# A state-space convolution beside a feed-forward: raw buffers of their own, a gate block in two halves, and loads ahead for the last convolution step

## The chip, the cores and the metric

The kernel runs on one NeuronCore of a Trainium2 chip. Five engines run their own instruction streams in order: TensorE (PE; its weight loads are shown apart as PEld), VectorE (DVE), ScalarE (ACT), GpSimd (POOL) and SyncE (SP), which here only issues DMAs. The metric is device time in microseconds. The measured times of the kernel before are 1185.72, 1187.77 and 1189.12 us, median 1187.77 us.

## The reference

The input u has 2048 rows of 576 channels, in float32. Each row is layer-normalised to xn. Two branches read xn, and the result is their sum with the input:

```python
x = A_u
xn = _layernorm(x, axis=-1)
return x + _A_ref(xn, ...) + _B_ref(xn, B_w1, B_w2)
```

Branch A is a long convolution. For each channel a kernel K of 2048 taps is built from 128 complex exponentials (`K = einsum("dn,dnl,dn->dl", C, exp(dt*A*l), dt*B).real`), K and xn are padded to 4096, multiplied in the frequency domain and transformed back, and `xn * Dskip` is added. Branch B is a feed-forward layer, `silu(xn @ w1) @ w2`, with 4608 hidden units.

## The kernel before

**Numbers.** Products are made at more than one float32r pass: an operand is split into a high part (a copy rounded to float32r, on ACT) and a low part (the subtraction of the two, on DVE), and three matmuls (high x high, high x low, low x high) make one product. The code names the parts h and l (`w1h`, `w1l`, `w2h`, `w2l`, `xh`, `xl`, `gh`, `gl`).

**Phase 0** (`phase0`, `norm`, `normed`, `put_xt`). The 2048 rows are 16 tiles of 128, j = 0 to 15. For each pair of tiles x is loaded (L156), the statistics are made on DVE (L170, L171), a power on POOL (L175) gives the inverse deviation, and xn is written by DVE for even j (L179) and by ACT for odd j (L184). PE transposes xn (L118, L122); ACT and DVE write the split transposed tiles (L119, L120, L123, L124). Four tiles make a block of 512 tokens with its `xts` entry: j = 0 to 3 are block b=0, j = 4 to 7 block b=1 of the first half. The tiles 8 to 15 are transposed too and kept in DRAM (`dxt`) for the second half. xn itself goes to DRAM (`dxn`) for the convolution.

**Feed-forward** (`ffn`). The hidden units are nine chunks of four tiles (FT = 4). For each half of the tokens and each chunk there are two blocks of 512 tokens, 36 blocks in all. `load_w1` and `load_w2` load weights in pairs of tiles, through a raw buffer (`w1r`, `w2r`, one of each), and split them. `up(blk, t)` makes one tile of the gate: 14 matmuls of 512 columns into a PSUM bank (L262 to L264), SiLU on ACT (L268), the copy to `gh` (L269) and the subtraction to `gl` (L270). `down(blk, jj)` makes one token tile of the output: 24 matmuls of 288 columns (L285) and two additions into `acc[j]` on DVE (L288). After the first half, `acc` of j = 0 to 7 is stored in DRAM as `dr0`, and the buffers take x of j = 8 to 15.

**Convolution** (`side`). `natural` and `kgen` build K, `spread` transforms xn, and their results lie in DRAM (`d1k`, `d1u`). `spectral` makes 32 steps of products (L628) and stores each to `d2` (L600). The last step is `add_conv(j, dst)`: it loads `ys` from `d2` in two DMAs (L635; a `ys` needs rows of all 32 spectral steps), makes eight small matmuls into two PSUM banks (`py`, L645; in the trace each shows as more than one record) and adds them to the destination on DVE (L651). For j = 0 to 7 this is done in `tail`: a buffer `r0` is loaded from `dr0` (L606; the trace names it r), `add_conv` adds to it, and it is stored to the output in four DMAs (L161). For j = 8 to 15 `add_conv` is called in `down` of the last chunk and adds to `acc[j]`, which is stored at the very end.

**Order.** The program is traced as one list by `weave`, which runs the feed-forward as the main line, of 288 steps (one for each `up` or `down`), and puts each piece of the side line at the step given by its mark, a fraction of 288. The marks (L655) are 0.14 to 0.65 for the kernel and `spread`, 0.65 to 0.88 for `spectral`, and then to 0.94 for `tail`. A scheduler then gives each engine its order: earlier traced work goes first among what it takes to be ready by its own times. `tc.high_priority()` moves work ahead of all other, and `behind(ins)` keeps what is traced in its block, on the engine of `ins` alone, behind `ins` in that engine's order; it waits for no data. Buffers of a pool tag are limited by `bufs`; a tile waits until its buffer is free. SP issues its DMAs in the order given, so one that waits holds those behind it. `pins` keeps the instructions that `behind` refers to: `xt_s` and `xt_v` are the last ACT copy and DVE subtraction of a transposed tile (L123, L124).

Of the kernel before, what the change touches and what calls it, by code (L numbers as in the profile page):

```python
# [10 lines left out]
F32 = mybir.dt.float32  # L11
# [30 lines left out]
def kernel(  # L42
# [83 lines left out]
    xts = {}  # L126
    pins = {}

    def spread(up):
# [29 lines left out]
    def store(t, j, engines):  # L159
        for ps, v, eng in quarters(ov, engines):  # L160
            eng.dma_start(v[:, j], t[ps])  # L161
# [55 lines left out]
    def behind(ins):  # L217
        return tc.issue_after(ins) if ins is not None else nullcontext()

    def ffn():  # L220
        w2v = w2.rearrange("(t p) d -> p t d", p=P)
        blocks = [(half, c, b) for half in range(2) for c in range(NCH) for b in range(2)]
# [1 line left out]

        def load_w1(half, c, t):
            f = c * FT + t
            r1 = wp.tile([P, 5, 2 * P], F32, tag="w1r", name="w1r", bufs=1)
            fs = slice(f * P, (f + 2) * P)
            nc.sync.dma_start(r1[:, 0:4, :], w1[0:512, fs].rearrange("(k p) f -> p k f", p=P))
            nc.sync.dma_start(r1[0:64, 4, :], w1[512:576, fs])  # L230
            nc.sync.dma_start(r1[64:128, 4, :], w1[512:576, fs])
            for i in range(2):
                h1 = wp.tile([P, 5, P], F32R, tag="w1h", name="w1h", bufs=FT + 1)
                l1 = wp.tile([P, 5, P], F32R, tag="w1l", name="w1l", bufs=FT + 1)
                src = r1[:, :, i * P:(i + 1) * P]
                nc.scalar.copy(h1, src)  # L236
                with behind(pins["xt_v"] if f == half == 0 else None):
                    nc.vector.tensor_sub(l1, src, h1)  # L238
                W1[half, c, t + i] = h1, l1

        def load_w2(half, c, t):
            f = c * FT + t
            r2 = wp.tile([P, 2, D], F32, tag="w2r", name="w2r", bufs=1)
            nc.sync.dma_start(r2, w2v[:, f:f + 2, :])
            for i in range(2):
                h2 = wp.tile([P, D], F32R, tag="w2h", name="w2h", bufs=FT + 1)
                l2 = wp.tile([P, D], F32R, tag="w2l", name="w2l", bufs=FT + 1)
                with behind(pins["xt_s"] if f == half == 0 else None):
                    nc.scalar.copy(h2, r2[:, i, :])  # L249
                with behind(pins["xt_v"] if f == half == 0 else None):  # L250
                    nc.vector.tensor_sub(l2, r2[:, i, :], h2)  # L251
                W2[half, c, t + i] = h2, l2
                yield

        def up(blk, t):
            half, c, b = blk
            xh, xl, x4 = xts[2 * half + b]
            h1, l1 = W1[half, c, t]
            ph = ps1.tile([P, 512], F32, tag="ps1", name="ph")
            for n, (w, v) in enumerate(((h1, xh), (h1, xl), (l1, xh))):  # L260
                for kt in range(NKT):
                    nc.tensor.matmul(ph, w[:, kt, :], v[:, kt, :], start=n + kt == 0, stop=False)  # L262
            nc.tensor.matmul(ph, h1[:, 4, :], x4, start=False, stop=False)  # L263
            nc.tensor.matmul(ph, l1[:, 4, :], x4, start=False, stop=True)  # L264
            gf = gp.tile([P, 512], F32, tag="gf", name="gf", bufs=2)
            gh = gp.tile([P, 512], F32R, tag="gh", name="gh")
            gl = gp.tile([P, 512], F32R, tag="gl", name="gl")
# [3 lines left out]
            G[blk, t] = gh, gl  # L271

        def down(blk, jj):
            half, c, b = blk
            j = 8 * half + 4 * b + jj
            js = slice(jj * P, (jj + 1) * P)
            if half == 1 and c == NCH - 1:
                add_conv(j, acc[j])
            for h in range(2):
                hs = slice(h * HD, (h + 1) * HD)  # L280
                po = ps2.tile([P, 512], F32, tag="ps2", name="po")
                n = 0
                for t in range(FT):
                    for g, w in ((0, 0), (0, 1), (1, 0)):
                        nc.tensor.matmul(po[:, :HD], G[blk, t][g][:, js], W2[half, c, t][w][:, hs],  # L285
                                         start=n == 0, stop=n == 3 * FT - 1)
# [18 lines left out]

        for t in (0, 2):
            load_w1(0, 0, t)
            for _ in load_w2(0, 0, t):
                pass
        yield 0  # L310
        for t in range(FT):
            up(blocks[0], t)
            yield 3.0

        for i, blk in enumerate(blocks):
# [20 lines left out]
                    if k in (0, 2) and more and b == 0:  # L336
                        load_w1(*new, k)

    kl = yp = None
    kf = {}  # L340

    def natural(nat):
# [259 lines left out]

    def tail():
        for j in range(8):
            r0 = yp.tile([P, D], F32, tag="r0", name="r0")
            nc.sync.dma_start(r0, dr0[j * P:(j + 1) * P, :])  # L606
# [16 lines left out]
    def mm3(dst, terms, hs):  # L623

        n = 0
        for sh, sl, (mh, ml) in terms:
            for st, mv in ((sh, mh), (sh, ml), (sl, mh)):
                nc.tensor.matmul(dst, st, mv[:, hs], start=n == 0, stop=n == 3 * len(terms) - 1)  # L628
                n += 1

    def add_conv(j, dst):

        ys = yp.tile([P, 4, HD], F32, tag="ys", name="ys")
        for h in range(2):
            nc.sync.dma_start(ys[64 * h:64 * h + 64],  # L635
                              d2[j * 256:(j + 1) * 256, h * HD:(h + 1) * HD].rearrange("(q r) d -> r q d", q=4))
        first = None
        py = [pss.tile([P, 512], F32, tag="pss", name="py") for _ in range(2)]
        for q1 in range(2):
            for q2 in range(2):  # L640
                for h in (1, 0):
                    o = 64 * q1 + 32 * q2
                    rows = slice(64 * h, 64 * h + 64)
                    with tc.high_priority(), behind(first):
                        mm = nc.tensor.matmul(py[h][o:o + 32, :HD], s4[rows], ys[rows, 2 * q2 + q1],  # L645
                                              start=True, stop=True,
                                              tile_position=(64 * h, o), skip_group_check=True)
                    first = first or mm.ins
        for h in range(2):
            hs = slice(h * HD, (h + 1) * HD)  # L650
            nc.vector.tensor_add(dst[:, hs], py[h][:, :HD], dst[:, hs])  # L651

    def side():
        nonlocal s4, kl, yp
# [34 lines left out]

        def at_mark(at):  # L690
            k = int(at)
            return marks[k] + (at - k) * (marks[k + 1] - marks[k]) if k < 3 else marks[3]

        with tc.tile_pool(name="kl", bufs=2) as kl:
            for at in spectral():
# [92 lines left out]
```

## Time and profile before

| what | value |
|---|---|
| measured times, us | 1185.72, 1187.77, 1189.12; median 1187.77 |
| the profiled execution, us | 1184.91, of which the span is 1183.1 |
| mean granted TensorE clock | 0.987 |
| busy PE, DVE, ACT, POOL, us | 1132.1, 942.5, 699.0, 24.7 |
| first and last matmul start, us | 10.68, 1178.6 |
| last spectral store landed, first `ys` issued, us | 1096.0, 1096.84 |
| HBM read and written, MB | 102.63, 44.90 |

Times within the profile are microseconds from the start of the span. A busy PE is one that has a matmul in flight: matmuls are pipelined, so the start-to-start distance of neighbours is what one more of them costs, and the duration of one is longer. Where a row of a timeline holds several instructions (xN), its time reaches from the first start to the last end, and may hold waits. A wait is put down to what came last. The row of the granted clock is in tenths of full speed, over 40 equal slices of the span.

### The profile page before, as it was taken

Reading aid. Unit: us, or ns where it says so; the run is one execution under the profiler, and the core shown is the slowest. Engines: PE = TensorE matmul, PEld = TensorE weight load, DVE = VectorE, ACT = ScalarE, POOL = GpSimd, SP = SyncE. Lnnn points to the kernel's source line nnn. Section 1 sums busy time; section 2 is a strip of 40 time slices with the busy share of each in tenths; the row PEclk is TensorE's granted clock in tenths of the full one; section 3 lists DMA queues with packets and bytes.
Section 4 is the critical chain, followed back from the end, with each engine's and each line's share of the span. In section 5 each row is a group of like instructions: output and inputs, shape, how many; then the busy total and the mean of one; then the engine's idle time right before and its main releaser. Section 6 shows DMA issues by size and latency. Waiting matters only on the chain.

```text
span 1183.1 us, 22598 instructions
## 1 busy us (share of the span) xinstructions
PE 1132.1 (96%) x8984; PEld 1014.9 (86%) x8984; DVE 942.5 (80%) x1645; ACT 699.0 (59%) x1246; POOL 24.7 (2%) x42
## 2 busy tenths in 40 slices
PE   5999999999999999999999999999999999999958
PEld 3898889888888898998898889899989999999726
DVE  5798898999888989999899985488767878876223
ACT  3465556566565657665665654477767777776200
POOL 1100000000000000000000000000000000000000
PEclk9999999999999999999999999999999999999969
DMA  9356220505124242447451413654544544440895
GB/s 266 117 158 202 78 85 21 132 31 120 62 84 89 93 89 93 89 155 211 153 132 47 124 47 94 167 165 145 151 128 146 154 142 145 151 148 31 214 245 132
DMA packets 161625, 148.92 MB, mean 126 GB/s; under 512 B 82448, under 2 KB 124192, under 8 KB 161008
## 3 DMA queue, kind: packets, MB, share of 16 engines
q1 hardware_dynamic: 157088, 132.19, 39.7%
q0 software_dynamic: 3472, 13.53, 4.0%
q10 hardware_dynamic: 960, 1.77, 0.6%
q8 instruction: 70, 1.15, 0.4%
q14 instruction: 35, 0.29, 0.1%
HBM read 102.63 MB, written 44.90 MB: 125 GB/s over the span
## 4 chain that ended last, share of the span: by engine, by line
PE 65%; DMA 12%; DVE 11%; ACT 6%; issue 3%; SPq 2%; POOL 0%; ACTq 0%; DVEq 0%; POOLq 0%
PE po L285 27%; PE ph L262 23%; DMA w1r<-in_B_w_dram 3%; DMA d1u<-u 2%; PE kp L530 2%; DMA ys<-d 2%; PE pk L628 2%; PE pb L628 2%; PE pu L628 2%; PE z L542 2%; PE ph L263 2%; PE ph L264 2%; DVE acc L288 1%; DVE S L509 1%; DVE C L509 1%
## 5 line engine op out<-in xcount | busy, mean ns | idle before, releaser
L285 PE MATMUL po<-w2h,gh 128*128 128x288 f32 x1152 | 337.7, 299 | 6.8 <-ACT gh L269 5.9
L285 PE MATMUL po<-w2l,gh 128*128 128x288 f32 x1152 | 339.6, 297 | 0.4 <-issue 0.4
L285 PE MATMUL po<-w2h,gl 128*128 128x288 f32 x1152 | 333.9, 297 | 1.4 <-DVE gl L270 1.4
L285 PEld LDWEIGHTS po<-w2h,gh 128*128 128x128 f32 x1152 | 216.5, 189 | 16.9 <-ACT gh L269 6.8
L285 PEld LDWEIGHTS po<-w2l,gh 128*128 128x128 f32 x1152 | 217.8, 189 | 6.4 <-issue 2.0
L285 PEld LDWEIGHTS po<-w2h,gl 128*128 128x128 f32 x1152 | 215.7, 189 | 4.9 <-DVE gl L270 2.2
L262 PE MATMUL ph<-xh,w1h 128*128 128x512 f32 x576 | 161.6, 396 | 4.7 <-ACT gf L268 2.7
L262 PE MATMUL ph<-xl,w1h 128*128 128x512 f32 x576 | 160.2, 391 | 0.0
L262 PE MATMUL ph<-xh,w1l 128*128 128x512 f32 x576 | 159.8, 392 | 0.0
L288 DVE TENSOR_TENSOR acc<-po,acc 128x288 f32<-128x288 f32 x288 | 125.6, 451 | 28.4 <-PE po L285 27.1
L262 PEld LDWEIGHTS ph<-xh,w1l 128*128 128x128 f32 x576 | 107.0, 188 | 22.3 <-issue 1.4
L268 ACT ACTIVATE gf<-ph 128x512 f32<-128x512 f32 x144 | 85.7, 596 | 68.2 <-PE ph L264 43.9
L262 PEld LDWEIGHTS ph<-xl,w1h 128*128 128x128 f32 x576 | 106.7, 188 | 20.7
L262 PEld LDWEIGHTS ph<-xh,w1h 128*128 128x128 f32 x576 | 104.2, 189 | 23.2 <-ACT gf L268 3.7
L269 ACT CAST gh<-gf 128x512 fp32r<-128x512 f32 x144 | 88.1, 620 | 48.5 <-PE po L285 46.6
L270 DVE TENSOR_TENSOR gl<-gf,gh 128x512 fp32r<-128x512 f32 x144 | 97.9, 684 | 18.0 <-ACT gh L269 17.2
L236 ACT CAST w1h<-w1r 128x640 fp32r<-128x640 f32 x72 | 51.6, 724 | 72.6 <-DMA w1r<-in_B_w_dram 64.8
L238 DVE TENSOR_TENSOR w1l<-w1r,w1h 128x640 fp32r<-128x640 f32 x72 | 58.7, 820 | 25.1 <-ACT w1h L236 24.8
L249 ACT CAST w2h<-w2r 128x576 fp32r<-128x576 f32 x72 | 46.5, 672 | 26.3 <-DMA w2r<-in_B_w_dram 21.5
L251 DVE TENSOR_TENSOR w2l<-w2r,w2h 128x576 fp32r<-128x576 f32 x72 | 52.6, 751 | 8.9 <-ACT w2h L249 8.5
L489 ACT ACTIVATE c<-th,magic 128x1040 f32<-128x1040 f32 x36 | 41.9, 1165 | 29.9 <-DVE C L510 22.0
L264 PE MATMUL ph<-x,w1l 128*128 128x512 f32 x144 | 56.6, 393 | 0.0
(169 smaller groups left out, 1845.2 us busy)
## 6 DMA issues: line engine op xcount, KB each, us to landing
w2r<-in_B_w_dram SPq DMA_DIRECT2D x36, 576.0 KB, 3.9
w1r<-in_B_w_dram SPq DMA_DIRECT2D x36, 512.0 KB, 4.7
d1u<-u SPq DMA_DIRECT2D x32, 288.0 KB, 2.6
d1k<-stage SPq DMA_DIRECT2D x18, 512.0 KB, 8.0
ur<-d1u SPq DMA_DIRECT2D x32, 288.0 KB, 3.7
kr<-d1k SPq DMA_DIRECT2D x32, 288.0 KB, 2.9
d<-yo SPq DMA_DIRECT2D x32, 288.0 KB, 3.9
ys<-d SPq DMA_DIRECT2D x32, 288.0 KB, 5.6
```

Of the source, the lines that this page charges most:

```text
L236: nc.scalar.copy(h1, src)
L238: nc.vector.tensor_sub(l1, src, h1)
L249: nc.scalar.copy(h2, r2[:, i, :])
L251: nc.vector.tensor_sub(l2, r2[:, i, :], h2)
L262: nc.tensor.matmul(ph, w[:, kt, :], v[:, kt, :], start=n + kt == 0, stop=False)
L264: nc.tensor.matmul(ph, l1[:, 4, :], x4, start=False, stop=True)
L268: nc.scalar.activation(gf, ph, AF.Silu)
L269: nc.scalar.copy(gh, gf)
L270: pins["gl"] = nc.vector.tensor_sub(gl, gf, gh).ins
L285: nc.tensor.matmul(po[:, :HD], G[blk, t][g][:, js], W2[half, c, t][w][:, hs], start=n == 0, stop=n == 3 * FT - 1)
L288: nc.vector.tensor_add(acc[j][:, hs], po[:, :HD], acc[j][:, hs])
L628: nc.tensor.matmul(dst, st, mv[:, hs], start=n == 0, stop=n == 3 * len(terms) - 1)
```

## The change

- `load_w1` and `load_w2`: for the first chunk of the first half, the second pair (t = 2) takes its raw buffer from phase 0's pool `pa`, so it does not share with the first pair. The first pair's three w1 DMAs are issued by POOL instead of SP. Both w1 pairs are traced before both w2 pairs. The w1l subtractions of these pairs come behind the last DVE instruction of tile j = 1 (before: those of the first pair behind tile 3's), the w2h copies behind tile 3's last ACT copy for both pairs, and the w2l subtractions behind the last w1l.
- `up` takes a range of columns, and the first block is done as two halves, columns 0 to 255 of all four tiles and then 256 to 511 of all four.
- In `side`, the DVE work of tiles 4 to 7 comes behind the last DVE instruction of tile 3 (`pins["xt3"]`).
- `add_conv` no longer loads: `conv_load(j)` does, two steps ahead, into four buffers instead of three, and `tail_load` loads `r0` two steps ahead into three. The `py` matmuls lose their high priority; the first of each step comes behind the last feed-forward matmul traced (`pins["pe"]`).
- The marks become 0.14, 0.65, 0.875, 0.905, 0.945: `spectral` ends at 0.875, and step j of `tail` is traced at 0.905 + 0.005 j.

```diff
@@ load_w1, load_w2
-            r1 = wp.tile([P, 5, 2 * P], F32, tag="w1r", name="w1r", bufs=1)
+            first = half == 0 and f < FT
+            r1 = (pa if first and t else wp).tile([P, 5, 2 * P], F32, tag="w1r", name="w1r", bufs=1)
...
-            nc.sync.dma_start(r1[:, 0:4, :], w1[0:512, fs].rearrange("(k p) f -> p k f", p=P))
-            nc.sync.dma_start(r1[0:64, 4, :], w1[512:576, fs])
-            nc.sync.dma_start(r1[64:128, 4, :], w1[512:576, fs])
+            eng = nc.gpsimd if first and t == 0 else nc.sync
+            eng.dma_start(r1[:, 0:4, :], w1[0:512, fs].rearrange("(k p) f -> p k f", p=P))
+            eng.dma_start(r1[0:64, 4, :], w1[512:576, fs])
+            eng.dma_start(r1[64:128, 4, :], w1[512:576, fs])
...
-                with behind(pins["xt_v"] if f == half == 0 else None):
-                    nc.vector.tensor_sub(l1, src, h1)
+                with behind(pins["xt1"] if first else None):
+                    pins["w1l"] = nc.vector.tensor_sub(l1, src, h1).ins
...
-            r2 = wp.tile([P, 2, D], F32, tag="w2r", name="w2r", bufs=1)
+            r2 = (pa if first and t else wp).tile([P, 2, D], F32, tag="w2r", name="w2r", bufs=1)
...
-                with behind(pins["xt_v"] if f == half == 0 else None):
+                with behind(pins["w1l"] if first else None):
                     nc.vector.tensor_sub(l2, r2[:, i, :], h2)
@@ up
-        def up(blk, t):
+        def up(blk, t, a=0, e=512):
...
-                    nc.tensor.matmul(ph, w[:, kt, :], v[:, kt, :], start=n + kt == 0, stop=False)
+                    nc.tensor.matmul(ph, w[:, kt, :], v[:, kt, a:e], start=n + kt == 0, stop=False)
...
@@ down
             if half == 1 and c == NCH - 1:
+                conv_load(j + 2)
                 add_conv(j, acc[j])
@@ ffn
         for t in (0, 2):
             load_w1(0, 0, t)
+        for t in (0, 2):
             for _ in load_w2(0, 0, t):
                 pass
         yield 0
         for t in range(FT):
-            up(blocks[0], t)
+            up(blocks[0], t, 0, 256)
+        for t in range(FT):
+            up(blocks[0], t, 256, 512)
             yield 3.0
@@ tail
         for j in range(8):
-            r0 = yp.tile([P, D], F32, tag="r0", name="r0")
-            nc.sync.dma_start(r0, dr0[j * P:(j + 1) * P, :])
-            add_conv(j, r0)
-            store(r0, j, (nc.sync,))
-            yield 2 + (j + 1) / 8
+            if j < 2:
+                conv_load(j)
+                r0s[j] = tail_load(j)
+        for j in range(8):
+            yield 3 + j / 8
+            if j < 6:
+                r0s[j + 2] = tail_load(j + 2)
+            conv_load(j + 2)
+            add_conv(j, r0s[j])
+            store(r0s[j], j, (nc.sync,))
+
+    def tail_load(j):
+        r0 = yp.tile([P, D], F32, tag="r0", name="r0", bufs=3)
+        nc.sync.dma_start(r0, dr0[j * P:(j + 1) * P, :])
+        return r0
@@ add_conv
+    def conv_load(j):
+        if j < NJ:
+            yss[j] = yp.tile([P, 4, HD], F32, tag="ys", name="ys", bufs=4)
+            for h in range(2):
+                nc.sync.dma_start(yss[j][64 * h:64 * h + 64],
+                                  d2[j * 256:(j + 1) * 256, h * HD:(h + 1) * HD].rearrange("(q r) d -> r q d", q=4))
...
-                    with tc.high_priority(), behind(first):
+            with behind(first):
...
@@ side
-        marks = (0.14, 0.65, 0.88, 0.94)
+        marks = (0.14, 0.65, 0.875, 0.905, 0.945)
         with tc.tile_pool(name="pa", bufs=4) as pa:
             for js in ((0, 1), (2, 3), (4, 5), (6, 7)):
-                phase0(pa, js)
+                with behind(pins["xt3"] if js[0] > 2 else None):
+                    phase0(pa, js)
+                pins[f"xt{js[1]}"] = pins["xt_v"]
```

More of the change, by code (lines that the diff above doesn't have):

```diff
@@ L127, with behind @@
     pins = {}
+    def behind(ins):
+        return tc.issue_after(ins) if ins is not None else nullcontext()
     def spread(up):
@@ L242, in load_w2 @@
             f = c * FT + t
-            r2 = wp.tile([P, 2, D], F32, tag="w2r", name="w2r", bufs=1)
+            first = half == 0 and f < FT
+            r2 = (pa if first and t else wp).tile([P, 2, D], F32, tag="w2r", name="w2r", bufs=1)
             nc.sync.dma_start(r2, w2v[:, f:f + 2, :])
@@ L247, in load_w2 @@
                 l2 = wp.tile([P, D], F32R, tag="w2l", name="w2l", bufs=FT + 1)
-                with behind(pins["xt_s"] if f == half == 0 else None):
+                with behind(pins["xt_s"] if first else None):
                     nc.scalar.copy(h2, r2[:, i, :])
-                with behind(pins["xt_v"] if f == half == 0 else None):
+                with behind(pins["w1l"] if first else None):
                     nc.vector.tensor_sub(l2, r2[:, i, :], h2)
@@ L284, in down @@
                     for g, w in ((0, 0), (0, 1), (1, 0)):
-                        nc.tensor.matmul(po[:, :HD], G[blk, t][g][:, js], W2[half, c, t][w][:, hs],
-                                         start=n == 0, stop=n == 3 * FT - 1)
+                        pins["pe"] = nc.tensor.matmul(po[:, :HD], G[blk, t][g][:, js], W2[half, c, t][w][:, hs],
+                                                      start=n == 0, stop=n == 3 * FT - 1).ins
                         n += 1
@@ L629, in mm3 @@
                 n += 1
-    def add_conv(j, dst):
[L633 to L637, printed above, removed]
-        py = [pss.tile([P, 512], F32, tag="pss", name="py") for _ in range(2)]
[L639 to L643, printed above, removed]
-                    with tc.high_priority(), behind(first):
[L645 to L648, printed above, removed]
+    def conv_load(j):
[4 more added lines that the diff above has]
+                                  d2[j * 256:(j + 1) * 256, h * HD:(h + 1) * HD].rearrange("(q r) d -> r q d", q=4))
+    def add_conv(j, dst):
+        ys = yss.pop(j)
+        py = [pss.tile([P, 512], F32, tag="pss", name="py") for _ in range(2)]
+        first = pins["pe"]
+        for n in range(8):
+            q1, q2, h = n // 4, n // 2 % 2, 1 - n % 2
+            o = 64 * q1 + 32 * q2
+            rows = slice(64 * h, 64 * h + 64)
+            with behind(first):
+                mm = nc.tensor.matmul(py[h][o:o + 32, :HD], s4[rows], ys[rows, 2 * q2 + q1],
+                                      start=True, stop=True, tile_position=(64 * h, o), skip_group_check=True)
+            if n == 0:
+                first = mm.ins
         for h in range(2):
@@ L691, in at_mark @@
             k = int(at)
-            return marks[k] + (at - k) * (marks[k + 1] - marks[k]) if k < 3 else marks[3]
+            return marks[k] + (at - k) * (marks[k + 1] - marks[k])
         with tc.tile_pool(name="kl", bufs=2) as kl:
```

21 lines of the change are left out of this document (10 added, 11 removed).

## The prediction

> **What bounds the kernel now.** I read the page's summary and slices first, then PE's waits, then windows over the two ends, then the chain and SP's own queue in the last 90 us. The summary and the slices:
>
> ```profile
> PE 1132.1 (96%) x8984; PEld 1014.9 (86%) x8984; DVE 942.5 (80%) x1645; ACT 699.0 (59%) x1246; POOL 24.7 (2%) x42
> ...
> PE   5999999999999999999999999999999999999958
> ...
> PEclk9999999999999999999999999999999999999969
> ```
>
> PE is the bound except in the first slice and the last two. It idles 1183.1 - 1132.1 = 51 us, and the change touches both places where the idle time is dense. PE's waits, whole run:
>
> ```profile
> PE py L645 <- DMA ys<-d: 14.6, 6, 7.7
> PE pt L118 <- DVE xn L179: 10.8, 2, 10.7
> ...
> PE ph L262 <- ACT w1h L236: 2.0, 1, 2.0
> ```
>
> The largest is the last convolution step waiting for its loads; the second is the start, before any x is normalised; the third shown is the second weight pair. Windows over both ends (span of window, busy PE, PEld, DVE, ACT, POOL with counts, granted clock, DMA share, GB/s):
>
> ```profile
> 1096.50:1166.20 69.70, 53.63 (x432) 36.55 (x430) 21.08 (x46) 9.61 (x16) 0.00 (x0) 0.85 0.91 226
> 1166.20:1183.10 16.90, 12.58 (x102) 11.28 (x102) 4.91 (x11) 0.00 (x0) 0.00 (x0) 1.00 0.26 71
> 1130.00:1150.00 20.00, 10.76 (x93) 5.20 (x86) 5.39 (x13) 0.00 (x0) 0.00 (x0) 0.50 0.96 231
> 10.68:20.00 9.32, 8.09 (x26) 5.29 (x27) 7.78 (x25) 6.24 (x14) 1.25 (x2) 1.00 1.04 317
> 20.00:40.00 20.00, 17.29 (x95) 14.59 (x94) 12.70 (x25) 10.55 (x20) 0.85 (x2) 1.00 0.70 211
> ```
>
> From 1096.5 (d2 complete, first ys load) to 1166.2 (last ys landed) PE is idle 16.1 us and the DMA engines are already 0.91 busy; after 1166.2 PE still has 102 matmuls, 12.6 us. SP's queue and the chain there:
>
> ```profile
> 1106.18 2.26 SPq L161 DMA_DIRECT2D out_dram<-r  x4
> ...
> 1113.46 0.35 SPq L606 DMA_DIRECT2D r<-dr  x1
> 1113.90 0.58 SPq L635 DMA_DIRECT2D ys<-d  x1
> ...
> 1121.89 0.58 SPq L635 DMA_DIRECT2D ys<-d  x1
> ...
> 1128.23 9.71 SPq L161 DMA_DIRECT2D out_dram<-r  x12
> ```
>
> ```profile
> 1108.13 5.32 DMA out_dram<-r
> ...
> 1123.79 5.54 DMA ys<-d
> ...
> 1140.47 6.06 DMA ys<-d
> ...
> 1159.67 6.49 DMA ys<-d
> ...
> 1168.89 10.01 PE po L285 x74
> ```
>
> SP stands from 1108.4 to 1113.5 for a store to land (the r0 buffer), then issues the two halves of one ys 8 us apart with 12 stores between, then twelve more stores in 9.7 us. Here ys loads are late because SP's order mixes them with stores, and PE, in order, stands behind them.
>
> **The change, part by part.** The sum is made against the profiled execution: 1184.91 us, span 1183.1 and 1.8 around it. It lies 2.9 below the median of 1187.77; I apply the difference to the median.
>
> *Buffers of their own, both w1 loads first.* Before, the second w1r is issued at 21.89, when the first raw buffer is free, and PE waits 2.0 us for its copy. Now both are loaded at once: the wait goes. The three first-pair DMAs leave SP (0.41+0.57+0.58 us of its queue) for POOL, whose only earlier DMA took 0.68; three end near 4 us, ahead of POOL's first pow at 7.63. The w1l subtractions (0.82 each) now follow j=1's x4 instead of j=3's at 20.00; the w2l ones (0.7) follow w1l.
>
> *Later statistics for j=4..7.* Eight bn_stats of 0.41 to 0.44 and their small followers move behind j=3 on DVE: 3.4 us out of 14.67 to 19.3, so j=3's subtract (19.29) can come about 2 us earlier. DMAs are not held by this, since the order binds DVE alone. What is late next: x of block b=1, done at 39 us before; DVE is busy 12.7 of 20 us from 20 to 40, so the moved 3.4 us fit.
>
> *First gate block in two halves.* 56 matmuls of 512 columns become 112 of 256. Start to start is 0.227 us at 512 columns (1118.97 to 1119.19 and its neighbours) and 0.132 at 288 (po rows). The line through both gives 0.1185 at 256; half of 0.227 is the lower end, 0.132 the upper. Extra: 56 x (0.237-0.227) = 0.56 us, between 0 and 2.1. I take 0.56, as 256 is near 288. ACT and DVE get twelve more instructions of about half size; both have room (ACT 10.55 of 20). In return PE can begin gate work when j=0,1 are transposed (j=1's copy ends at 14.03) instead of 17.64.
>
> PE's idle time from 10.68 to 40 is 1.23+2.71 = 3.94 us: that is the most that these three edits can return. I take three quarters, 2.95, less the 0.56.
>
> *Contention at the start.* w1 on POOL begins near 2 us instead of 4.23, while x for j=0..3 is still landing (the chain has it until 8.43), and DVE's xn at 10.07 stands behind statistics that wait for that x. No row shows the sharing. From 0 to 10 us 230 GB/s are moved; 655 KB at that rate are 2.8 us, the upper end; none is the lower. 2.2 us earlier at half share is 0.25 MB, 1.1 us: I take 1.0. Start in all: -2.95+0.56+1.0 = -1.4 us (bounds -3.9 to +4.9).
>
> The Trainium skill (DMA: Bandwidth & Descriptors, Issuing engines are not separate DMA queues) says that DMAs of SP, ACT and GpSimd run on the same engines and interleave, and only issue time is saved. By that rule the whole 2.8 would be paid and the start would be +0.4; shares of 0.85 and 1.04 in the first 20 us fit it.
>
> *Loads ahead in the last step.* 32 ys DMAs (0.58 each), 8 r0 loads (0.45) and 32 r stores (0.43) stay; SP needs 36 us of 70 for them either way. ys gets a fourth buffer, and ys and r0 are traced two steps ahead of the store that used to precede them. If DMA stays full, the same bytes need 0.91 x 69.7 = 63.4 us: at best 6.3 us come off the last landing. I take 5, since SP's stand of 5 us and its long store runs are what the loads now pass. A loss is not excluded: the other end is +6 (R1 below).
>
> *No priority for py, order behind the last matmul traced.* For j=0..7 that pin costs nothing: at 1100 there are left 195 po matmuls (8.1 steps of 24) and 62 of L262 (5.2 steps of 12), so the feed-forward stands at step 274.7 of 288, past every mark of the tail (0.905 to 0.94 x 288 = 261 to 271). For j=8..15 py(j) now comes behind all po of j-1, so a late ys no longer holds po that is ready. Of 12.6 us PE work after the last landing, 24 po x 0.132 and a py of 0.7 must remain, 3.9; up to 8.7 can go, none at worst. I take 3: closer to none, as py rows at 1146 to 1168 show PE already mixing both.
>
> The clock was 0.50 from 1130 to 1150, and the rows around 1146 show py at 1.32 against 0.71 warm. Most of that lies inside the waits, so I count it nowhere else. The trace lost the clock after gaps of 1.4 and 2.0 us (1124.6 to 1129.5). The Trainium skill (TensorE: Matmul & The Clock Gate, What's actually happening) puts the loss at an idle window of about 3.4 us; by that rule, gaps cut to 2 us would keep the clock and give up to 2.7 us more, by the row they would not. The row decides.
>
> *Marks.* Spectral steps are traced 0.005 x 288 = 1.4 steps earlier. As it ends 19 steps behind its mark of 253 already, it runs at its own chain's pace (10.4 us a step). 0, bounds +-4.6 (1.4 x 3.2). The middle, 40 to 1096: 16 us of scattered PE stalls can shuffle; 0, bounds +-3.
>
> Sum: -1.4 - 5 - 3 = -9.4. 1184.91 - 9.4 = 1175.5 profiled, 1178.4 against the median; I say 1178.
>
> **The rivals.**
> *R1, slower: the r0 reload in front of ys.* In traced order SP has store(j), r0(j+3), ys(j+3); r0 has three buffers, so it waits for store(j) to land. A step is then 1.7 (store) + 3.3 (median landing) + 0.45 + 1.2 = 6.65 us; from 1105 (first store ready) ys8 is issued at 1105 + 6 x 6.65 = 1145 and lands 5.6 later, near 1150, against 1144.3 before: +6, none of the 3, start -1.4: 1192.4. It decides when a store lands in more than about 2.3 us with SP in that order. For: the stand of 5 us until 1113.5. Against: ys3 was put ahead of a waiting r0 before (1105).
> *R2, no change: DMA is the bound.* A share of 0.91 counts as full; only the start remains: 1186.4.
> *R3, everything fits.* 6.3 + 8.7 off the tail, 1.4 at the start: 1171.4. Against: ys and d of each j have near equal cost (0.59+0.29 MB at 226 GB/s is 3.9 us; 24 po and py 3.9), so any jitter shows.
> *R4, the whole w1 load comes ahead of x.* Start +0.4, tail -8: 1180.2. For: DVE's wait for x until 8.43.
>
> **How the numbers follow.** Forecast 0.40, R1 0.20, R2 0.17, R3 0.13, R4 0.10. A measurement of this kernel tells about 0.3% (3.6 us) from no change. Faster: 0.40+0.13+0.10 and a quarter of R2 = 0.67; same 0.13; slower 0.20. The forecast's own range, with half the bounds of the tail and the middle, is 1173 to 1184. From 1169 to 1191 leaves out about half of R1 and a part of R3.
>
> **What would show it.** First L262 near 14 us with 256 columns; no wait of PE for w1h; idle from 10.68 to 40 below 2 us; first transposes no later than 11.7. In the tail: ys<-d waits of PE below 6 us, last ys landed near 1160, DMA share about 0.97, fewer than 80 matmuls after it. It is wrong if SP stands for out_dram<-r at every step, if xn comes after 12, or if d2 is complete several us away from 1095.

## The result and the profile after

The changed kernel takes 1178.93 us (median of 4 runs, 1173.75 to 1179.79) against 1187.86 us before in the same comparison (median of 4): ratio 0.9927, 95% interval 0.9898 to 0.9956, which is 8.7 us less (5.2 to 12.1). The forecast was 1178. The profiled execution took 1179.79 us, the slowest of the four, with a span of 1178.0, against a span of 1183.1 before.

The summary and the slices of the changed kernel:

```profile
PE 1139.1 (97%) x9040; PEld 1020.8 (87%) x9040; DVE 943.0 (80%) x1649; ACT 701.9 (60%) x1254; POOL 27.3 (2%) x45
...
PE   6999989999999999999999999999999999999988
...
PEclk9999989999999999999999999999999999999979
```

PE idles 1178.0 - 1139.1 = 38.9 us where it idled 51, and the next to last slice went from 5 to 8. Its waits:

```profile
PE pt L118 <- DVE xn L182: 10.4, 2, 8.8
PE po L290 <- DVE acc L293: 7.3, 7, 2.5
...
PE py L669 <- DMA ys<-d: 2.4, 2, 1.7
```

The wait for `ys` fell from 14.6 to 2.4 us and the wait for `w1h` is gone. Another wait grew in part of their place: `po` behind DVE's additions into `acc`, 7.3 us in 7 waits, where it was 1.0 us in 2. The windows over both ends of the changed kernel (columns as before):

```profile
8.81:40.00 31.19, 29.24 (x207) 27.99 (x208) 25.59 (x64) 20.45 (x44) 2.26 (x3) 1.00 0.64 216
...
1096.53:1160.00 63.47, 57.28 (x418) 39.74 (x417) 20.07 (x45) 9.46 (x16) 0.00 (x0) 0.89 0.93 236
1160.00:1164.50 4.50, 4.50 (x46) 3.87 (x45) 2.71 (x7) 0.00 (x0) 0.00 (x0) 1.00 0.92 249
1164.50:1178.00 13.50, 9.56 (x86) 7.43 (x84) 4.05 (x10) 0.00 (x0) 0.00 (x0) 1.00 0.32 82
```

At the start PE is busy from 8.81 and idles 1.95 us up to 40. After d2 is complete (1096.53, where the first `ys` is issued) PE idles 6.2 us up to 1160. But the loads of `ys` did not come earlier. The line for the issues of tile `ys` before (count, duration in ns, first and last issue):

```profile
L635 SPq DMA_DIRECT2D ys<-d x32: 573/580/681, 1096.8 to 1159.7; - x32
```

And the same line of the changed kernel:

```profile
L656 SPq DMA_DIRECT2D ys<-d x32: 573/580/644, 1096.5 to 1159.3; - x32
```

Before, the last `ys` is issued 62.9 us after the first; in the changed kernel 62.8. Loading ahead moved the last load nothing forward; PE waits less, probably because it has other work meanwhile. Four pieces of the chain of the changed kernel (start, duration):

```profile
1118.18 2.96 DMA out_dram<-r
...
1132.53 4.37 DMA ys<-d
...
1157.83 4.57 PE po L290 x33
...
1170.69 3.38 PE po L290 x24
```

The chain goes mostly through transfers up to 1137 and through PE, with 2 us of DVE, at the end, where before it had a load of `ys` as late as 1159.67. SP's waits from 1096.53 on (us in all, times, longest):

```profile
SPq L164 <- DVE acc L293: 7.8, 3, 3.6
SPq L164 <- DMA ys<-d: 6.7, 9, 1.6
SPq L656 <- DMA ys<-d: 5.6, 6, 1.5
SPq L629 <- DMA out_dram<-r: 4.8, 6, 1.3
```

The last of them in a stretch of SP's queue:

```profile
1118.18 1.88 SPq L164 DMA_DIRECT2D out_dram<-r  x4
1121.22 0.34 SPq L629 DMA_DIRECT2D r<-dr  x1
...
1124.81 1.81 SPq L164 DMA_DIRECT2D out_dram<-r  x4
1126.66 0.58 SPq L656 DMA_DIRECT2D ys<-d  x1
1127.35 0.54 SPq L164 DMA_DIRECT2D out_dram<-r  x1
1130.11 0.34 SPq L629 DMA_DIRECT2D r<-dr  x1
```

Each reload of `r0` (L629) that needs a used buffer stands behind a store that has to land first: SP issues nothing from 1120.06 to 1121.22 and from 1127.89 to 1130.11, and waits for stores are part of both stretches. Before, the same wait was 4.6 us, in one piece.

### The profile page after: what moved, and what is told of

The parts are those of the page before. It is cut to its first block, busy times and chain, and to the rows that moved or that the text cites. A ratio compares the mean times of both kernels' runs of the same rounds, so it can differ in the third digit from the quotient of the medians.

```text
span 1178.0 us, 22743 instructions
## 1 busy us (share of the span) xinstructions
PE 1139.1 (97%) x9040; PEld 1020.8 (87%) x9040; DVE 943.0 (80%) x1649; ACT 701.9 (60%) x1254; POOL 27.3 (2%) x45
## 4 chain that ended last, share of the span: by engine, by line
PE 55%; DVE 16%; DMA 14%; ACT 8%; issue 4%; SPq 2%; POOL 0%; ACTq 0%; DVEq 0%
PE po L290 24%; PE ph L266 18%; DMA w1r<-in_B_w_dram 3%; DMA w2r<-in_B_w_dram 2%; PE kp L539 2%; DVE acc L293 2%; DMA d1u<-u 2%; PE z L551 2%; PE pb L649 2%; PE ph L268 1%; PE pu L649 1%; PE ph L267 1%; PE pk L649 1%; DMA dxt<-xt 1%; DVE S L518 1%
## 5 line engine op out<-in xcount | busy, mean ns | idle before, releaser
L290 PE MATMUL po<-w2h,gh 128*128 128x288 f32 x1152 | 339.0, 301 | 12.2 <-DVE acc L293 7.3
L290 PEld LDWEIGHTS po<-w2h,gh 128*128 128x128 f32 x1152 | 216.5, 189 | 26.5 <-DVE acc L293 11.7
L266 PE MATMUL ph<-xh,w1h 128*128 128x512 f32 (+1 forms) x592 | 164.2, 394 | 1.4 <-ACT gf L273 1.4
L266 PE MATMUL ph<-xl,w1h 128*128 128x512 f32 (+1 forms) x592 | 163.5, 391 | 0.0
L266 PE MATMUL ph<-xh,w1l 128*128 128x512 f32 (+1 forms) x592 | 159.6, 386 | 0.0
L273 ACT ACTIVATE gf<-ph 128x512 f32<-128x512 f32 (+1 forms) x148 | 86.3, 583 | 92.1 <-PE ph L268 52.3
L266 PEld LDWEIGHTS ph<-xl,w1h 128*128 128x128 f32 x592 | 110.1, 192 | 22.0 <-issue 0.9
L275 DVE TENSOR_TENSOR gl<-gf,gh 128x512 fp32r<-128x512 f32 (+1 forms) x148 | 98.5, 671 | 20.7 <-ACT gh L274 20.0
L274 ACT CAST gh<-gf 128x512 fp32r<-128x512 f32 (+1 forms) x148 | 88.8, 608 | 36.3 <-PE po L290 34.7
L254 DVE TENSOR_TENSOR w2l<-w2r,w2h 128x576 fp32r<-128x576 f32 x72 | 52.7, 751 | 16.4 <-ACT w2h L252 16.1
L268 PE MATMUL ph<-x,w1l 128*128 128x512 f32 (+1 forms) x148 | 57.3, 387 | 0.0
L500 ACT ACTIVATE c<-th 128x1040 f32<-128x1040 f32 x36 | 38.6, 1074 | 30.9 <-DVE th L499 30.8
```

The costliest lines, as they stand in the source:

```text
L266: nc.tensor.matmul(ph, w[:, kt, :], v[:, kt, a:e], start=n + kt == 0, stop=False)
L268: pins["pe"] = nc.tensor.matmul(ph, l1[:, 4, :], x4[:, a:e], start=False, stop=True).ins
L290: pins["pe"] = nc.tensor.matmul(po[:, :HD], G[blk, t][g][:, js], W2[half, c, t][w][:, hs], start=n == 0, stop=n == 3 * FT - 1).ins
```

## The experiments

All times are set against runs of the kernel before in the same comparison, on the same chip; the median of before was 1186.39, 1182.79 or 1188.06 us in the three comparisons of the experiments, so kernels of different comparisons are compared by their ratios. The ratio and its interval are the comparison's own estimate, not the quotient of two medians; the column us is what the ratio makes of the median before, and differs from the difference of the medians by up to 2 us. d2 is taken as complete when the first `ys` is issued; "gate left" counts the gate matmuls (`ph`) from there on, and "last ys" and "end" are counted from there too. "Reload" is SP's wait for `out_dram<-r` in front of the loads of `r0`.

| kernel | ratio, 95% | us | d2 complete | gate left | last ys | reload | end |
|---|---|---|---|---|---|---|---|
| before | 1 | 0 | 1096.8 | 85 | 62.9 | 4.6 | 86.3 |
| changed | 0.9927, 0.9898-0.9956 | -8.7 | 1096.5 | 97 | 62.8 | 4.8 | 81.5 |
| changed, again | 0.9922, 0.9895-0.9948 | -9.2 | 1093.7 | 97 | 62.4 | 4.7 | 81.6 |
| start alone | 0.9923, 0.9892-0.9953 | -9.1 | 1092.4 | 96 | 65.3 | 5.6 | 83.8 |
| last step alone | 0.9974, 0.9958-0.9990 | -3.1 | 1099.7 | 86 | 61.0 | 7.8 | 82.3 |
| priority back | 0.9938, 0.9916-0.9961 | -7.4 | 1088.3 | 97 | 61.1 | 4.9 | 87.9 |
| no loads ahead | 0.9882, 0.9858-0.9906 | -14.0 | 1090.1 | 96 | 57.7 | none | 79.2 |
| order alone | 1.0017, 0.9999-1.0034 | +2.0 | 1099.5 | 85 | 68.1 | 10.0 | 87.8 |
| whole first block | 0.9970, 0.9949-0.9991 | -3.5 | 1095.1 | 88 | 60.9 | 6.8 | 81.9 |
| statistics free | 0.990, 0.987-0.993 | -11.8 | 1086.7 | 97 | 63.0 | 4.6 | 84.3 |
| first w1 by SP | 0.9974, 0.9954-0.9993 | -3.1 | 1099.0 | 86 | 59.6 | 7.1 | 80.8 |
| few stores | 0.9871, 0.9845-0.9896 | -15.3 | 1093.7 | 97 | 52.9 | 10.8 | 77.1 |
| no loads ahead, stores on ACT | 0.9927, 0.9902-0.9952 | -8.7 | 1087.5 | 96 | 52.4 | 6.7 | 80.4 |
| no loads ahead, statistics free | 0.9862, 0.9837-0.9887 | -16.4 | 1092.4 | 96 | 58.6 | none | 80.3 |

The profile columns are of one execution each. Seven of these kernels (changed, the same again, start alone, priority back, no loads ahead, and the two with other stores) have the same order of instructions on every engine up to the last step; yet their d2 is complete anywhere from 1087.5 to 1096.5. A difference of 3 us between two single profiles therefore says nothing; the counts and the sums over several kernels do.

### Which end of the kernel the gain is from

*Start alone*: all edits of the start, with `tail`, `add_conv` and the marks as before.

```diff
-                conv_load(j + 2)
                 add_conv(j, acc[j])
...
-            with behind(first):
+                    with tc.high_priority(), behind(first):
...
-        marks = (0.14, 0.65, 0.875, 0.905, 0.945)
+        marks = (0.14, 0.65, 0.88, 0.94)
```

> The edits at the start (raw buffers, both w1 loads first, half blocks, later statistics) with the last step as before. Theory A (the start only lets the feed-forward run ahead, and the end is set by the convolution line): d2 complete within 2 us of 1096, time within 3 us of before, so 1185 to 1190. Rival B (PE is the bound, so what the start saves reaches the end): the 4.7 us that the changed kernel is ahead at 40 us come off, 1182 to 1184.

It gives 1176.94 us against 1186.39, -9.1 us (-12.8 to -5.6): the start alone measures as much as the whole change, and more than either theory allowed.

*Last step alone*: the kernel before with the new `tail`, `conv_load`, `add_conv` and marks.

```diff
-            ph = ps1.tile([P, 512], F32, tag="ps1", name="ph")[:, a:e]
+            ph = ps1.tile([P, 512], F32, tag="ps1", name="ph")
...
-                with behind(pins["xt3"] if js[0] > 2 else None):
-                    phase0(pa, js)
+                phase0(pa, js)
```

> The edits at the last step (loads ahead, no priority, order behind the last traced matmul, marks) with the start as before. Theory A: nearly all of the gain, 1178 to 1183. Rival B: the gain of the changed kernel less 4.7 us, so 1183 to 1186.

It gives 1183.43 against 1186.39, -3.1 us (-5.0 to -1.2), just inside Rival B's range. The sum of the two, -12.2, is more than the whole, but within their intervals. On a kernel with the new start the edits of the last step show no gain: -9.1 without them, -8.7 and -9.2 with them.

*Changed, again*: the changed kernel without an edit, in the comparison that also holds first w1 by SP, whole first block and statistics free.

> The changed kernel itself once more, beside the others on one chip. If the parts add (start alone -9, last step alone -3), it comes to 1173 to 1176 where before is 1186; if they share one gain, 1176 to 1180.

1175.64 against 1182.79, -9.2 us: nearly the same ratio in another comparison, and no sign that the parts add up to -12.

### The last step

*Priority back*: the changed kernel with the old order of `py`.

```diff
-        first = pins["pe"]
+        first = None
...
-            with behind(first):
+            with tc.high_priority(), behind(first):
```

> The changed kernel, with py at high priority again and not behind the last traced matmul; loads stay two steps ahead. Theory C (late loads are the loss, and loads ahead cure it): within 2 us of the changed kernel, 1177 to 1181, PE's waits on ys below 5 us. Rival D (the order on PE is what matters): 4 us or more of the gain are lost, 1183 to 1188, PE's waits on ys above 8 us again.

1177.99 against 1186.39: -7.4 us, not to be told from the changed kernel by its time, as Theory C has it; but PE waits 8.0 us for `ys`, which is nearer to Rival D. Its profile has 41.0 us from the first addition for tile 8 to the end, where the changed kernel has 34.0. In the three profiles with priority (before, start alone, this one) that stretch is 38.8 us on the mean (37.4 to 41.0), and in the ten without it that have SP store `r0` 35.4 (34.0 to 37.1).

*Order alone*: the kernel before, only with `py` behind the last feed-forward matmul instead of at high priority, and three `ys` buffers.

```diff
-        first = None
+        first = pins["pe"]
...
-                    with tc.high_priority(), behind(first):
+                    with behind(first):
```

> The kernel before with one edit only: py loses its priority and comes behind the last feed-forward matmul traced; loads, buffers, marks and the start as before. Theory J (PE's order is the whole gain of the last step: from the first py of tile 8 to the end 35 us without the priority against 39 with it): 3 to 4 us faster than before, that stretch below 36 us. Rival K (it takes the loads ahead as well): within 1.5 us of before.

1189.09 against 1188.06, +2.0 us (-0.1 to +4.0): no gain, so Theory J is out. The stretch from tile 8 on is 34.3 us, as in the others without priority, but the stretch ahead of it grew from 48.9 to 53.5. PE's wait for `ys` is 16.4 us, against 14.6 before:

```profile
PE py L645 <- DMA ys<-d: 16.4, 4, 9.6
```

*No loads ahead*: the changed kernel with `ys` and `r0` loaded in their own step. Four `ys` buffers and the new order stay.

```diff
-            if j < 2:
-                conv_load(j)
-                r0s[j] = tail_load(j)
-        for j in range(8):
             yield 3 + j / 8
-            if j < 6:
-                r0s[j + 2] = tail_load(j + 2)
-            conv_load(j + 2)
+            r0s[j] = tail_load(j)
+            conv_load(j)
...
-                conv_load(j + 2)
+                conv_load(j)
                 add_conv(j, acc[j])
```

> The changed kernel, with ys and r0 loaded in their own step again (r0 first), four ys buffers kept, py without priority. Theory C: at least 4 us lost, 1183 to 1190, last ys landing after 1163. Rival D: within 2 us of the changed kernel, 1177 to 1181, as PE has po to do while ys is late.

1173.54 against 1186.39, -14.0 us: without the loads ahead the kernel is not slower, as Theory C had it, nor the same, as Rival D had it, but by its ratio faster. SP's longest waits from 1090.08 on:

```profile
SPq L164 <- DVE acc L293: 8.3, 3, 3.5
SPq L651 <- DMA ys<-d: 7.2, 9, 1.4
SPq L164 <- DMA ys<-d: 6.9, 9, 1.2
SPq L164 <- DVE r L670: 2.7, 3, 1.1
```

A stretch of its queue that answers to the one shown above:

```profile
1112.27 1.85 SPq L164 DMA_DIRECT2D out_dram<-r  x4
1114.23 0.36 SPq L624 DMA_DIRECT2D r<-dr  x1
1114.63 0.58 SPq L651 DMA_DIRECT2D ys<-d  x1
1115.98 1.71 SPq L164 DMA_DIRECT2D out_dram<-r  x4
1117.79 0.38 SPq L624 DMA_DIRECT2D r<-dr  x1
```

No wait for `out_dram<-r` is left: with three buffers the load of tile j needs the store of tile j - 3, where two steps ahead the load of tile j + 2 needs that of tile j - 1, the one just issued. Here each reload follows the stores ahead of it at once. The last `ys` is issued 57.7 us after the first instead of 62.8, by the line of its issues:

```profile
L651 SPq DMA_DIRECT2D ys<-d x32: 573/582/714, 1090.1 to 1147.8; - x32
```

*Few stores*: the changed kernel with one of the four stores of each `r0`, so that three quarters of that output are missing.

```diff
-            store(r0s[j], j, (nc.sync,))
+            ps, v, eng = next(quarters(ov, (nc.sync,)))
+            eng.dma_start(v[:, j], r0s[j][ps])
```

> The changed kernel with three of the four stores of each r0 left out for tiles 0 to 7 (so three quarters of that output are missing): 1.77 MB and 24 issues of SP less. Theory L (from d2 complete to tile 8 the DMA engines set the pace): the first py addition into acc comes 6 to 8 us earlier after d2, near 40 us instead of 47, and the end 5 to 8 us earlier than the changed kernel. Rival M (the waits of PE and DVE on each other do): less than 3 us in both.

1172.21 against 1188.06, -15.3 us. With 1.8 MB less to store the last `ys` is issued at 52.9 and the first addition for tile 8 starts 40.9 us after d2 is complete, against 47.5, which is Theory L's forecast. So the stores hold the loads of this stretch. But the edit takes 24 issues out of SP's queue together with the bytes, and does not tell the one from the other. SP waits longer for the reloads here (10.8 us), and its loads are early all the same.

*No loads ahead, stores on ACT*: the kernel without loads ahead, with the stores of `r0` issued by ACT.

```diff
-            store(r0s[j], j, (nc.sync,))
+            store(r0s[j], j, (nc.scalar,))
```

> Loads in their own step as in the no-ahead run, and the r0 stores issued by ACT instead of SP, so that no load stands behind a store in SP's order. Theory L: within 2 us of the no-ahead run, 12 to 15 us faster than before. Rival N (SP's order is the pace): 4 us or more faster than that, 17 us or more faster than before.

1177.72 against 1188.06, -8.7 us, with runs from 1169.70 to 1184.06: neither Theory L's time nor Rival N's. Its profile, of the fastest run, has the last `ys` at 52.4 and tile 8 at 38.4, but 42.0 us from there to the end: what the loads gained did not shorten the end. Why these runs spread so was not followed. The window from d2 to the landing of its last `ys` (columns as before):

```profile
1087.53:1145.50 57.97, 50.54 (x381) 35.15 (x380) 18.52 (x40) 8.33 (x14) 0.00 (x0) 0.94 0.99 269
```

All bytes are stored here, and the last `ys` is issued as early as with few stores. At 269 GB/s more is moved than in the other windows shown of this stretch (226 to 247). So bytes alone do not set the pace in the kernels whose stores SP issues; the place of the stores in SP's queue has a share in it. How large it is stays open.

### The start

*First w1 by SP*: the changed kernel with the first w1 pair issued by SP again.

```diff
-            eng = nc.gpsimd if first and t == 0 else nc.sync
+            eng = nc.sync
```

> The changed kernel with the first w1 pair loaded by SP as before. If the POOL queue takes bandwidth from x (the prediction's 1.0 us), the first transpose comes at or before 8.8 us and the time is 0 to 1 us better. If it only saves SP's issue time, the second w1 pair and w2 come about 1.6 us later, the first transpose stays at 8.8, and the time is within 2 us.

1181.44 against 1182.79, -3.1 us: about 6 us of the change's 9 are lost, where 2 at most were expected. DVE's timeline in this kernel (start, duration, source line), around the first xn:

```profile
8.29 0.82 DVE L173 BATCH_NORM_STATS2 st<-acc 128x6 f32<-128x288 f32 x2 [0.94 <-DMA acc<-in_A_u_dram]
...
9.80 0.57 DVE L182 TENSOR_SCALAR xn<-acc,mv,sd 128x576 f32<-128x576 f32 x1
```

The timeline of the changed kernel, with its first gate matmul:

```profile
8.18 0.58 DVE L182 TENSOR_SCALAR xn<-acc,mv,sd 128x576 f32<-128x576 f32 x1 [0.56 <-POOL sd L178]
...
9.00 1.54 DVE L173 BATCH_NORM_STATS2 st<-acc 128x6 f32<-128x288 f32 x4
...
14.13 2.06 PE L266 MATMUL ph<-xh,w1h 128*128 128x256 f32 x8
```

With SP as issuer the first xn stands behind the statistics of tiles 2 and 3, which wait for x until 8.29, as it did before (8.55, xn at 10.07). With POOL as issuer DVE's order has xn first, and PE's first transpose is at 8.81 instead of 10.43. By the traces the last x of tiles 2 and 3 lands at 8.2 to 8.5 us in the four kernels in which SP issues the first w1, and at 8.5 to 10.0 in the ten with POOL, 0.6 us later on the mean. In the changed kernel it has landed (8.52) before DVE comes to it at 9.00; in start alone and statistics free DVE waits for it until 9.22 and 9.53, and the xn of tile 2 follows at 12.87 and 13.18 instead of 12.72. The weights themselves come no earlier: POOL issues the first pair from 1.94 us on instead of 4.06, and its last piece lands at 10.04 against 9.74.

The Trainium skill (DMA: Bandwidth & Descriptors, Issuing engines are not separate DMA queues) says that transfers started by different engines interleave on the same DMA engines, so only issue time is saved; the later x, and weights that land no earlier, agree with it. The gain of this edit lies elsewhere: with another issuer DVE was given another order.

*Whole first block*: the changed kernel with the first gate block in 512 columns.

```diff
-            up(blocks[0], t, 0, 256)
-        for t in range(FT):
-            up(blocks[0], t, 256, 512)
+            up(blocks[0], t)
```

> The changed kernel with the first gate block in whole tiles of 512 columns. Theory F (the half block is what fills PE before 20 us): first gate matmul after 16 us, PE idle from 10 to 40 us above 2 us, 3 us or more lost against the changed kernel of the same call. Rival G (the raw buffers do it, as they take the waits at 26 to 38 us away): within 2 us of the changed kernel or up to 1 us faster, as 56 matmuls of overhead go.

1180.39 against 1182.79, -3.5 us: again about 6 us are lost, though the first gate matmul is only 3 us later and PE's idle time up to 40 us is 12.1 us against 10.8. Its first gate matmul in PE's timeline:

```profile
17.10 3.36 PE L266 MATMUL ph<-xh,w1h 128*128 128x512 f32 x7 [0.67 <-ACT xh L119]
```

The table has a part of the rest. Five kernels lack one of the edits that start PE early: before, last step alone, order alone, whole first block, first w1 by SP. They have 85 to 88 gate matmuls left when d2 is complete; the nine others have 96 or 97, without exception. Those eleven at 0.227 us are 2.5 us of PE work that was ahead of d2 and now lies in the stretch behind d2, where PE has idle time for it. With the same last step the stretch from d2 to the end is no longer for them: 81.5 and 81.6 us in the two profiles of the changed kernel, 80.8 to 82.3 in the three kernels with its last step and 86 to 88 gate matmuls left. That accounts for 2.5 of the 6 us, and the idle time for 0.5 to 1.3; the rest is not settled. As undoing either edit costs 6 of the 9 us, their worths do not add: the gain needs both.

*Statistics free*: the changed kernel without the order that holds the work of tiles 4 to 7.

```diff
-                with behind(pins["xt3"] if js[0] > 2 else None):
-                    phase0(pa, js)
+                phase0(pa, js)
```

> The changed kernel without the order that puts the statistics of tiles 4 to 7 behind tile 3. Theory F and G both: tile 3's subtract some 2 us later and 0 to 2 us lost. Rival H (this order is the main part of the start, since DVE gates every first step): 4 us or more lost.

1172.17 against 1182.79, -11.8 us: no expectation had it faster. The order is worth nothing, and leaving it out is if anything better than the changed kernel beside it (-9.2), with intervals that overlap.

### Both undone

*No loads ahead, statistics free*: the changed kernel with the two edits above taken out.

> The changed kernel without the loads ahead and without the order on the statistics of tiles 4 to 7, the two edits whose undoing gave the fastest runs. If both were real they add: 15 to 18 us faster than before. If the differences of 3 to 5 us between kernels with the same start are scatter of the executions, 9 to 13 us faster, like the rest.

1171.35 us against 1188.06, ratio 0.9862 (0.9837 to 0.9887), -16.4 us: the lowest ratio measured, as expected if the two add, below before and, as its interval ends at 0.9887, below the changed kernel too. Taking the loads ahead out gained 4.8 us from the changed kernel beside "changed, again" (-9.2 to -14.0), and 4.6 us from statistics free (-11.8 to -16.4). Each pair alone overlaps a little; both point the same way by about the same size. Neither pair was run in one comparison, and the medians themselves differ by 2.1 and 0.8 us only, so that the loads ahead gain nothing is well founded, and that they cost 5 us is less so.

## Why the prediction was right, and where it was not

The total was right (-9.4 against -8.7 and -9.2) by luck, as two errors nearly cancel: the start alone measured -9.1 where -1.4 was forecast, and the last step alone -3.1 where -8 was.

**Start, predicted -1.4 (bounds -3.9 to +4.9).** The step that failed here is the sum of the start, which priced idle time from 10.68 on and took the first transpose as it was. Alone it measured -9.1 (-12.8 to -5.6), past the bound. By the profiles: d2 is complete at 1098.7 on the mean of the three kernels with the old start, and at 1091.7 on the mean of the seven with the new one and the same order, 6.9 us earlier. Of that, 3.1 is PE's idle time up to 40 us (14.0 to 10.9), 2.5 the eleven gate matmuls that moved behind d2, and 2.1 idle time and lost clock in the middle (21.8 to 19.7, added up from windows of 20 us, which among the seven alone scatters by more than that), together 7.7, which is as near as these single profiles go. This is an account by size; no run isolates its terms.

- *Contention, +1.0*: it is there, 0.6 us on the mean, on x of tiles 2 and 3, but "DVE's xn at 10.07 stands behind statistics that wait for that x" no longer held, since the first xn came to stand ahead of them. The term is 0 in the changed kernel, where no statistics wait for x after the first xn; the first transpose came 1.87 us earlier instead.
- *Buffers of their own*: right; the 2.0 us wait is gone.
- *First gate block in two halves*: the spacing is 0.12 us, as the line gave, and the first gate matmul is at 14.13, as forecast. Its worth was read from the idle time at the start only; undoing it costs about 6 us.
- *Later statistics, j=3's subtract 2 us earlier*: wrong. The subtract is at 19.30 against 19.29, the last DVE work of tile 3 at 20.71 against 20.00, and taking the order out costs nothing. In DVE's timeline the four w1l subtractions, which the same change puts behind tile 1, stand at 14.94 for 3.03 us, where the statistics stood; the prediction named them and did not count them there.

**Middle 0 and Marks 0.** Start alone has the old marks and the same order as the changed kernel up to the last step, so the marks do nothing there: right. The middle was not 0: the shift of gate work behind d2 is what the prediction had no term for.

**Loads ahead, -5 (best -6.3, worst +6).** Wrong. The last `ys` is issued 62.8 us after the first as against 62.9, and taking the edit out brings 57.7 and 58.6, and no loss of time. "SP's stand of 5 us and its long store runs are what the loads now pass" is the step that failed: they don't pass them. With `r0` two steps ahead in three buffers a reload waits for the store just issued; SP stood 4.6 to 7.8 us for it in the seven profiles with the loads ahead and all stores, and not at all in no loads ahead and in the last kernel. That is the wait which R1 names. That this stand makes the loads late is not shown, and the table speaks against it as the whole cause: among those seven the longest stands (7.8 and 7.1 us) go with early last loads (61.0 and 59.6), and few stores and stores on ACT stand 10.8 and 6.7 us and are the earliest of all. Whether the loads ahead cost time, and by what in the order of the queue, stays open; a kernel with a fourth `r0` buffer would have tested the stand and was not run.

**No priority for py, -3.** The size after tile 8 is right: 38.8 to 35.4 us. But it is no gain by itself, as order alone shows (+2.0): what is saved behind tile 8 is lost ahead of it. In one comparison the kernel without loads ahead is 4.9 us faster than start alone, with intervals that overlap a little. It differs from that one by this order, the fourth `ys` buffer and the marks, which were not taken apart.

**The signs that were named.** Right: first gate matmul near 14 us with 256 columns, no wait for w1h, 1.95 us idle to 40, first transpose ahead of 11.7, 2.4 us of waits for `ys`. Wrong: the last landing near 1160 (issued at 1159.3, landed at 1163.5 by the trace), a DMA share near 0.97 (0.93), fewer than 80 matmuls after it (86 from 1164.5). Of the signs of being wrong, one came: SP stood for `out_dram<-r` at the reloads, and the total held all the same.

**The rivals.** R1's stand was there, in six waits of at most 1.3 us, but did not make the last step longer than before. R2 was right that the loads ahead gain nothing, but a share of 0.91 was not full: stores on ACT reached 0.99. The window of the kernel without loads ahead, from d2 to 6.1 us (the median to landing there) after its last `ys`, holds a share of 0.97:

```profile
1090.08:1153.90 63.82, 54.99 (x443) 39.46 (x447) 20.43 (x45) 9.47 (x16) 0.00 (x0) 0.95 0.97 247
```

R3's time of 1171.4 (-16.4) was reached only by the last experiment, with the loads ahead and the order on the statistics taken out, and not by R3's terms. R4 is out: the first transpose came earlier, not later.

## What to carry to other kernels

Loading ahead through a small set of buffers can put a wait into the queue: count how many steps lie between the store that frees a buffer and the load that needs it, and look in the queue's own waits for the stand. A shorter wait of the engine does not show that a load came earlier; check the load's first and last issue. Work that moves from in front of a stretch in which the engine idles into that stretch can be free, so the value of an earlier start is the earlier completion of what opens the stretch, not the idle time at the start alone. When a total comes out as predicted, run each part alone: here both halves were off by about five us or more.

## What the runs showed of the hardware

The same order of instructions on every engine gives different profiles: the first spectral product is anywhere from 747.7 to 754.7 us and d2 complete from 1087.5 to 1096.5, in seven profiles, while the stretch between the two is 337 to 342 us.

PE lost its clock in the changed kernel's last step at 1117.3, after gaps of 1.03 and 0.40 us from 1114.8 on, and stayed at half for ten us, though it was busy without a break from 1121.6 on. Windows of PE's clock there (third column from the right):

```profile
1114.00:1116.00 2.00, 0.97 (x5) 0.67 (x5) 0.23 (x1) 0.94 (x2) 0.00 (x0) 1.00 1.07 277
1116.00:1117.00 1.00, 0.60 (x4) 0.41 (x3) 1.00 (x2) 1.00 (x3) 0.00 (x0) 1.00 1.06 317
1117.00:1118.00 1.00, 0.67 (x9) 0.28 (x12) 1.00 (x4) 0.94 (x2) 0.00 (x0) 0.64 0.50 141
1118.00:1119.00 1.00, 1.00 (x16) 0.18 (x8) 0.53 (x1) 0.00 (x0) 0.00 (x0) 0.50 0.90 128
...
1122.00:1124.00 2.00, 2.00 (x13) 1.28 (x6) 0.52 (x2) 0.00 (x0) 0.00 (x0) 0.50 0.74 189
1124.00:1126.00 2.00, 2.00 (x10) 2.00 (x9) 0.82 (x2) 0.00 (x0) 0.00 (x0) 0.50 0.90 225
1126.00:1127.00 1.00, 1.00 (x6) 1.00 (x5) 0.00 (x0) 0.00 (x0) 0.00 (x0) 0.50 1.09 203
1127.00:1128.00 1.00, 1.00 (x18) 0.29 (x17) 0.00 (x0) 0.00 (x0) 0.00 (x0) 0.74 0.99 237
```

The Trainium skill (TensorE: Matmul & The Clock Gate, What's actually happening) puts the loss at one idle window of about 3.4 us and the return after about 3.4 us of sustained work. Here the measurement differs on the loss: no gap was longer than 1.03 us, and 1.43 us were idle in the 2.5 us before it. The return came 5.9 us after unbroken work began. In the clock records of the 14 traces, from 25 us on, every change lies on a grid of 3.41 us. Where PE had the full clock and was idle for less than 1.25 us of a grid window (by its modelled matmul ends), it kept it; where it was idle for more than 1.9 us, it lost it; between the two both are found.
